# Windowed attention with sink tokens, then a token-and-channel mixer: a new start for the first batch (ones products, masks on TensorE, early sink rows) and a new order of loads

## The chip, the cores and the metric

The kernel runs on one core of one Trainium2 chip. The metric is the device time of one execution in microseconds (us), the median of several runs. Five engines work at once, each through its own list of instructions in order: PE (TensorE, matrix products), ACT (ScalarE), DVE (VectorE), POOL (GpSimd) and SP (SyncE, which here only issues transfers). Transfers are issued by SP (the hardware queue, q1 in the profile) and by POOL (the software queue, q0).

## The reference

Four batches, 8 heads, 768 positions, head size 64. Attention sees a window of 128 positions and 4 sink tokens. Its output, 768 x 512 per batch, goes through a mixer over tokens and one over channels.

```python
def _attn_ref(q, k, v, n_sink, window):
    scores = (1.0 / np.sqrt(D)) * np.matmul(q, k.transpose(0, 1, 3, 2))
    rel = pos[:, None] - pos[None, :]
    keep = (pos[None, :] < n_sink) | ((rel >= 0) & (rel < window))
    a = softmax(np.where(keep, scores, -1e9))
    return np.matmul(a, v)
def _moe_ref(x, w_tok1, w_tok2, w_ch1, w_ch2):
    h = np.maximum(x.transpose(0, 2, 1) @ w_tok1, 0.0) @ w_tok2
    u = x + h.transpose(0, 2, 1)
    return u + np.maximum(u @ w_ch1, 0.0) @ w_ch2
```

## The kernel before

**Pairs.** Heads are taken two at a time: 16 pairs, four per batch. SP loads q and k of a pair in fp32 (`load_qk`, line 72), POOL or, for pair 0, DVE casts them to bf16, and POOL issues the load of v (`load_v`, line 101), which casts in the transfer. PE transposes q and k (`transpose_q`, `transpose_k`, line 111) and ACT or DVE evicts the results, k in two halves (`kTz`), the second after the first. `score(p, kt)` makes the scores of one tile of 128 keys against 256 queries for both heads, ACT takes the exponential, and the window mask is applied in one of two ways: DVE multiplies the exponentials with 0 and 1 (line 390), or PE adds a large negative number first, by a product of the identity with `mask_add` (line 374). In the first four pairs the tiles with odd `kt` use the second way. `score_sinks` scores the 4 sink rows (`kTs`, copied out of `kTz`) and `pv` multiplies with v and, for the sinks, with `v_sinks`, which `sink_rows` copies out of v.

**Mixer.** `mix_h` and `mix_u` mix tokens; DVE adds x to the result of `mix_u` (line 538). For batch 0 PE transposes u (`transpose_u`); for the others a DMA does. `mix_channels` has 24 `v1` units per batch (product with w_ch1, then relu) and 24 `out_part` units (product with w_ch2, then an add and a store).

**Order.** All engines' lists are written by a planner before the kernel runs (`Plan.run`). It holds two streams of PE units: main (attention and token mixing of batch 0, then the channel mixing of all batches) and side (attention and token mixing of batches 1 to 3). Each stream keeps its own order. The planner has a cost for every unit and a due time for every load (`LANDED`), takes the stream that can begin, and keeps side at a pace given by `target`: side work of the next batch is to be done when 85% of the main work of a batch is (for the first from 20% on). The due times only decide the order that is written; on the chip each instruction waits for its real operands, and what stands behind it on its engine waits too.

**Loads.** POOL issues, in this order: v of pairs 0 and 1, the casts of pairs 1 and 2, v of pairs 2 and 3, the cast of pair 3, both token weights, the four parts of w_ch1. Pair p + 4 is loaded when `pv` of pair p is through (`load_next`); loads of q and k also wait until the last weight load so far has landed (`held`).

Of the kernel before, what the change touches and what calls it, by code (L numbers as in the profile page):

```python
# [16 lines left out]
def kernel(  # L17
# [77 lines left out]
    NV = 4  # L95
# [37 lines left out]


# [3 lines left out]
    mask_add = singles.tile([P, 2, 2, P], BF16)  # L138
# [21 lines left out]
    kTs = [singles.tile([P, 2, D], BF16, name=f"kTs{n}") for n in range(NKB)]  # L160

    v_sinks = [singles.tile([P, 2, D1], BF16, name=f"v_sink{n}") for n in range(NKB)]
    vs[0], _ = load_v(0)
    vs[1], _ = load_v(1)
    for n in range(NKB):
        e = (nc.vector, nc.gpsimd)[n]
        in_order(e.memset(kTz[n][D:P, 0], 0.0))
        in_order(e.memset(kTz[n][0:D, 1], 0.0))
        in_order(e.memset(kTs[n], 0.0))
        in_order(e.memset(v_sinks[n], 0.0))  # L170
    in_order(nc.vector.tensor_copy(out=mask_first, in_=mask_main))
    in_order(nc.vector.memset(mask_first[0:n_sink], 1.0))
    in_order(nc.vector.tensor_scalar(
        out=mask_add, in0=mask_main, scalar1=-1.0, scalar2=30000.0, op0=ALU.add, op1=ALU.mult,
    ))
# [21 lines left out]

    cast_qk(3)
    load_w(w_tok1, moe_w_tok1.rearrange("(t p) n -> p t n", p=P))
    load_w(w_tok2, moe_w_tok2.rearrange("(t p) n -> p t n", p=P))  # L200
    for n in range(NW):
        held = load_ch1(n)
# [22 lines left out]
    class Plan:  # L225
# [27 lines left out]
        def other(self):  # L253
            best = None
            for n, op in enumerate(self.pending):
                r = self.ready(op)
                if r is None:
                    continue
                e = min(op.cost, key=lambda e: max(self.free[e], r) + op.cost[e])
                t = max(self.free[e], r)  # L260
                if best is None or t < best[0] - 1e-6:
                    best = (t, n, e)
            return best
# [56 lines left out]
    def transpose_q(p):  # L320
        key = ("qT", p)

        def run():
            tiles["ps_q", p] = bank("mx", NT, P, dtype=BF16)
            for j in range(NT):
                transpose(tiles["ps_q", p][:, j], bfs[p][0][:, j])

        def evict(e):
            t = att_pool.tile([P, P, NT], BF16, name="qT2")
            copy(e, t, tiles["ps_q", p].rearrange("d j p -> d p j"))  # L330
            tiles[key] = t.rearrange("d p j -> d (p j)")

        done[key] = Op({"DVE": 950.0, "ACT": 900.0}, evict)
        return unit(340, run, [done["q_bf", p]], "mx", [done[key]])

    def transpose_k(p):
        kz, ks = kTz[p % NKB], kTs[p % NKB]

        def run():
            tiles["ps_k", p] = bank("mx", NT, P, dtype=BF16)  # L340
            for j in range(NT):
                transpose(tiles["ps_k", p][:, j], bfs[p][1][:, j])
            del bfs[p]

        def evict(i):
            return lambda e: copy(
                e, kz[ds(D * i, D), i].rearrange("d (p j) -> d p j", j=NT),
                tiles["ps_k", p][ds(D * i, D)].rearrange("d j p -> d p j"),
            )


        old = [done["sk", p - NKB]] if p >= NKB else []
        first = Op({"ACT": 800.0, "DVE": 950.0}, evict(0), old)
        second = Op({"ACT": 800.0, "DVE": 950.0}, evict(1), [first])
        sinks = Op({"ACT": 220.0, "DVE": 200.0}, lambda e: copy(e, ks[:, :, 0:n_sink], kz[:, :, 0:n_sink]), [second])
        tiles["kTz", p] = kz
        done["kT", p], done["kTs", p] = second, sinks
        done["kT0", p] = first
        return unit(340, run, [done["k_bf", p]], "mx", [first, second, sinks], [first, second])

    def score(p, kt):
# [3 lines left out]
        pe_mask = p < NHP and kt % 2 == 1  # L365
        tag = "mx" if p < NHP and kt % 2 else "sc"

        def run():
            if kt == 0:
                tiles["pT", p] = pt_pool.tile([P, NT, 2, 2, P], BF16, name="pT")  # L370
            ps_s = tiles["ps_s", p, kt] = bank(tag, 2, 2 * P)
            if pe_mask:
                mm(
                    ps_s[:, :, 0:nq * P].rearrange("p i (n q) -> p i n q", q=P), ident, mask_add[:, :, 0:nq],
                    start=True, stop=False,
                )
            for i in range(2):
                mm(
                    ps_s[:, i, 0:nq * P], tiles["kTz", p][:, i, ts(kt, P)], tiles["qT", p][:, kt * P:(kt + nq) * P],
                    start=not pe_mask, stop=True,  # L380
                )

# [14 lines left out]
        return unit(220 * nq * (1 if not pe_mask else 2) / 2, run, [done["qT", p], done["kT", p]], tag, then, [x])  # L397

    def score_sinks(p):
        def run():  # L400
            tiles["pT_sink", p] = pt_pool.tile([P, (NT - 2) * P], BF16, name="pT_sink")
            tiles["ps_sk", p] = bank("sc", (NT - 2) * P)
            mm(
                tiles["ps_sk", p], kTs[p % NKB].rearrange("p i c -> p (i c)"), tiles["qT", p][:, 2 * P:],
                start=True, stop=True,
            )
# [8 lines left out]
    def pv(p, half):  # L415
        b, hp = pairs[p]
        tag = "mx" if p < NHP and half else "pv"
        vsk = v_sinks[p % NKB]
# [33 lines left out]
        if half:  # L452
            done["pv", p] = op
            if p + NHP < len(pairs):
                op.then += load_next(p)
        return op

    def sink_rows(p):
        def both(e):
            for i in range(2):  # L460
                copy(e, v_sinks[p % NKB][D * i:D * i + n_sink, i], vs[p][0:n_sink, i, 0])

        done["vs", p] = Op({"ACT": 440.0, "DVE": 400.0}, both, [done["v", p]] + ([done["pv", p - NKB]] if p >= NKB else []))
# [61 lines left out]
    def mix_u(b, g, s0, n):  # L525
        c0, cn = group(b, g)

        def run():
            ps_u = tiles["ps_u", b, g, s0] = bank("mx", n, cn)
            for st in range(n):  # L530
                for tt in range(NTOK):
                    mm(
                        ps_u[:, st], w_tok2[:, tt, ts(s0 + st, P)], tiles["mix", b][0][:, tt, c0:c0 + cn],
                        start=(tt == 0), stop=(tt == NTOK - 1),
                    )

        def add(e):
            in_order(nc.vector.tensor_tensor(  # L538
                out=u_part(b, g, s0, n), in0=tiles["ps_u", b, g, s0],
                in1=x_sb[b][:, s0:s0 + n, c0:c0 + cn], op=ALU.add,  # L540
            ))

        op = Op({"DVE": 150.0 + 1.05 * n * cn}, add)
        done["u", b, g, s0] = op
        return unit(n * NTOK * cn * 0.422, run, done["h", b, g] + [done["tok2"]], "mx", [op])
# [34 lines left out]
    def attention_and_tokens(b):  # L580
        p0 = b * NHP
        units = [transpose_q(p0), transpose_k(p0)]
        for p in range(p0, p0 + NHP):
# [14 lines left out]
            units[-1].then.append(sink_rows(p))  # L598
# [4 lines left out]
        if b == 0:  # L603
            units += [mix_h(b, 0, 0, 1), pv(p, 0), mix_h(b, 0, 1, 1), pv(p, 1)]
            for st in range(NT):
                units.append(mix_u(b, 0, st, 1))
                if st >= 2:
                    units.append(transpose_u(b, 0, st - 2, 1))
            units += [
                mix_h(b, 1, 0, NTOK), transpose_u(b, 0, NT - 2, 1), mix_u(b, 1, 0, 4), transpose_u(b, 0, NT - 1, 1),  # L610
                mix_u(b, 1, 4, 2), transpose_u(b, 1, 0, 4), transpose_u(b, 1, 4, 2),
            ]
# [71 lines left out]
    def load_next(p):  # L684
        nxt = p + NHP

        def load_w2(n):
            def run(e):
                nonlocal held
                held = load_ch2(n)  # L690
            return run

        ops = []
        if 2 <= p < NHP:
            for n in (2 * p - 4, 2 * p - 3):
                done["ch2", n] = Op({"Q": 2500.0}, load_w2(n), [], lag=LOAD_LAG)
                ops.append(done["ch2", n])
        def load(e):
            nonlocal held
            raws[nxt] = load_qk(nxt, held if p < NHP else None)  # L700
            vs[nxt], held = load_v(nxt)
            bfs[nxt] = cast_tiles()

        def cast(n):
            return lambda e: copy("POOL", bfs[nxt][n].rearrange("p j h d -> p h j d"), raws[nxt][n])

        done["v", nxt] = Op({"Q": 4000.0}, load, [done["pv", p]] + ops, lag=LOAD_LAG)
        ops.append(done["v", nxt])
        for n, name in enumerate(("q_bf", "k_bf")):
            done[name, nxt] = Op({"POOL": 850.0}, cast(n), [done["v", nxt]])  # L710
            ops.append(done[name, nxt])
        return ops


    LANDED = {"q_bf": [0, 8400, 10500, 14700], "k_bf": [0, 9500, 12000, 15500], "v": [14400, 16500, 18000, 19000]}
    for n in LANDED:
        for p in range(NHP):
            done[n, p] = landed(float(LANDED[n][p]))
    done["tok1"], done["tok2"] = landed(21000.0), landed(23000.0)
    for n in range(NW):  # L720
        done["ch1", n] = landed(26000.0 + 2500.0 * n)

    plan = Plan()
    plan.free.update(PE=3000.0, ACT=2200.0, DVE=3900.0, Q=30000.0)
    raw0 = raws.pop(0)
    for n, (name, at) in enumerate((("q_bf", 3900.0), ("k_bf", 5100.0))):
# [4 lines left out]
        plan.pending.append(done[name, 0])  # L731

# [14 lines left out]
    def target(m):  # L747
        m -= first
        total = 0.0
        for n, (msize, ssize) in enumerate(sizes):  # L750
            begin = 0.2 if n == 0 else 0.0
            f = (m / msize - begin) / (0.85 - begin)
# [44 lines left out]
```

## Time and profile before

| | |
|---|---|
| median of 3 runs | 227.07 us (226.96 to 228.21) |
| the profiled execution | 226.43 us, span 224.7 us |
| PE busy | 203.8 us (91%) |
| DVE, ACT, POOL busy | 130.1, 123.3, 53.0 us |
| granted TensorE clock | 1.000 (mean) |
| DMA moved | 28.59 MB, mean 127 GB/s |

The span runs from the first to the last instruction of the core; the profiled execution's own time is 1.7 us longer than its span, and 0.6 us under the median. Durations below are of this one execution. A matrix product is shown until its result is written, so products in a row overlap: what a product costs in a row of them is the distance from start to start. L108 and L111 are the lines of helpers (`mm`, `transpose`), so rows are told apart by their tiles: `ps_sc` and `ps_mx` are PSUM tiles, `pT` the exponentials, `u_sb` the mixed tokens, `o_sb` the output.

### The profile page before, as it was taken

The numbers are of one execution on the slowest core, as the hardware profiler recorded it, in microseconds if no ns is written. First come the engines' busy times: TensorE is split into PE (matmuls) and PEld (weight loads), VectorE is DVE, ScalarE is ACT, GpSimd is POOL, SyncE is SP. The second block draws the span as 40 slices with busy tenths as digits, with TensorE's granted clock in tenths as the row PEclk, the third lists the DMA queues.
The fourth block names the chain that finished last, engine by engine and source line by source line (L and its number), as shares of the span: only waits on it lengthen the run. The fifth ranks groups of instructions, "written<-read, shape, count | busy, mean of one in ns | idle before, by whom it ended". The sixth has DMA issues, their size and how long they took to land.

```text
span 224.7 us, 4298 instructions
## 1 busy us (share of the span) xinstructions
PE 203.8 (91%) x1716; PEld 131.5 (59%) x1716; DVE 130.1 (58%) x286; ACT 123.3 (55%) x248; POOL 53.0 (24%) x70
## 2 busy tenths in 40 slices
PE   1787897997996999699999999999999999999992
PEld 1456565674664656467776665667765664565440
DVE  6388974165997764468966544679846643000321
ACT  2788945895881511799872510889954311774000
POOL 8798106602534035000440152000000000000000
PEclk9999999999999999999999999999999999999999
DMA  6999997998977399940552999100004124100222
GB/s 195 311 188 155 203 192 238 159 162 282 303 44 100 74 252 271 247 147 3 36 35 48 266 226 166 74 0 3 0 3 117 47 96 117 47 3 0 93 95 93
DMA packets 51284, 28.59 MB, mean 127 GB/s; under 512 B 35392, under 2 KB 48192, under 8 KB 51264
## 3 DMA queue, kind: packets, MB, share of 16 engines
q0 software_dynamic: 29600, 7.08, 33.6%
q1 hardware_dynamic: 21664, 21.24, 30.6%
q8 instruction: 13, 0.21, 0.4%
q14 instruction: 7, 0.06, 0.1%
HBM read 26.74 MB, written 6.29 MB: 147 GB/s over the span
## 4 chain that ended last, share of the span: by engine, by line
PE 76%; DMA 11%; DVE 5%; ACT 4%; issue 1%; POOL 1%; SPq 0%; POOLq 0%
PE ps_mx L108 60%; PE ps_sc L108 8%; DMA w_ch<-in_moe_w_ch_dram 5%; PE ps_pv L108 5%; PE ps_mx L111 4%; DMA k_f<-in_k_dram 4%; ACT kTz L115 3%; DMA q_f<-in_q_dram 2%; DVE kTs L117 2%; DVE kTz L117 1%; ACT pT L384 1%; DVE o_sb L653 1%; DVE x_sb L440 0%; SPq L72 0%; POOL q_bf L117 0%
## 5 line engine op out<-in xcount | busy, mean ns | idle before, releaser
L108 PE MATMUL ps_mx<-uT,w_ch 128*128 128x384 bf16 x384 | 69.2, 326 | 0.0
L108 PE MATMUL ps_mx<-w_ch,v1T 128*128 128x512 bf16 x288 | 68.8, 379 | 0.0
L384 ACT ACTIVATE pT<-ps_sc 128x512 bf16<-128x512 f32 x84 | 45.7, 566 | 20.0 <-PE ps_sc L108 19.2
L108 PEld LDWEIGHTS <-w_ch 128*128 128x128 bf16 x384 | 36.7, 98 | 20.5
L108 PEld LDWEIGHTS <-v1T 128*128 128x128 bf16 x288 | 27.4, 98 | 26.2
L121 ACT ACTIVATE v1T<-ps_mx 128x384 bf16<-128x384 f32 x67 | 32.7, 491 | 16.1 <-PE ps_mx L108 8.1
L653 DVE TENSOR_TENSOR o_sb<-ps_mx,u_sb 128x512 f32<-128x512 f32 x24 | 16.5, 687 | 42.6 <-PE ps_mx L108 42.6
L108 PE MATMUL ps_sc<-qT,kTz 128*128 128x256 bf16 x168 | 30.4, 270 | 6.4 <-ACT kTz L115 3.6
L101 POOL DMA_DIRECT2D v_aug<-in_v_dram x16 | 16.9, 1056 | 55.6 <-ACT pT L384 19.1
L390 DVE TENSOR_TENSOR pT<-pT,mask_main 128x512 bf16<-128x512 bf16 (+1 forms) x68 | 28.7, 434 | 1.9 <-ACT pT L384 1.3
L108 PEld LDWEIGHTS <-kTz 128*128 128x128 bf16 x192 | 17.9, 101 | 18.3 <-ACT kTz L115 5.4
L123 DVE TENSOR_SCALAR v1T<-ps_mx 128x384 bf16<-128x384 f32 x29 | 16.1, 555 | 13.5 <-PE ps_mx L108 13.2
L108 PEld LDWEIGHTS <-w_tok 128*128 128x128 bf16 x192 | 17.7, 98 | 8.0 <-issue 2.7
L538 DVE TENSOR_TENSOR u_sb<-ps_mx,x_sb 128x512 bf16<-128x512 f32 (+2 forms) x26 | 15.4, 643 | 10.1 <-PE ps_mx L108 10.1
L108 PEld LDWEIGHTS <-pT 128*128 128x128 bf16 x352 | 16.8, 97 | 2.9 <-issue 0.7
L121 ACT ACTIVATE h1T<-ps_mx 128x512 bf16<-128x512 f32 (+2 forms) x9 | 5.0, 550 | 24.3 <-PE ps_mx L108 24.3
L115 ACT ACTIVATE kTz<-ps_mx 64x768 bf16<-64x768 bf16 x20 | 16.1, 802 | 1.4 <-PE ps_mx L111 0.6
L108 PE MATMUL ps_pv<-v_aug,pT 128*128 128x65 bf16 x304 | 16.3, 194 | 0.0
L115 ACT ACTIVATE qT<-ps_mx 128x768 bf16<-128x768 bf16 x9 | 7.3, 812 | 16.0 <-PE ps_mx L111 16.0
L440 DVE TENSOR_TENSOR x_sb<-ps_pv,recip 128x384 bf16<-128x384 f32 x28 | 15.5, 553 | 0.6
L117 POOL CAST q_bf<-q_f 128x768 bf16<-128x768 f32 x12 | 10.0, 834 | 24.7 <-DMA q_f<-in_q_dram 24.7
L111 PE MATMUL ps_mx<-ident,q_bf 128*128 128x128 bf16 x96 | 8.7, 231 | 6.9 <-DVE q_bf L117 4.5
(59 smaller groups left out, 192.2 us busy)
## 6 DMA issues: line engine op xcount, KB each, us to landing
q_f<-in_q_dram SPq DMA_DIRECT2D x16, 384.0 KB, 4.6
k_f<-in_k_dram SPq DMA_DIRECT2D x16, 384.0 KB, 5.4
out_dram<-o_sb SPq DMA_DIRECT2D x24, 256.0 KB, 2.2
v_aug<-in_v_dram POOLq DMA_DIRECT2D x16, 192.0 KB, 6.0
w_ch<-in_moe_w_ch_dram POOLq DMA_DIRECT2D x8, 384.0 KB, 8.9
w_tok<-in_moe_w_tok_dram POOLq DMA_DIRECT2D x2, 384.0 KB, 6.0
uT<-u_sb SPq DMA_TRANSPOSE x9, 3.2
```

Of the source, the lines that this page charges most:

```text
L101: d = in_order(nc.gpsimd.dma_start(out=v_aug.rearrange("p i t d -> p (i t) d")[:, :, 0:D], in_=v[b].rearrange("h s d -> (h s) d")[2 * hp * ...
L108: in_order(nc.tensor.matmul(*args, skip_group_check=True, **kwargs))
L111: in_order(nc.tensor.transpose(out, in_, ident))
L115: in_order(nc.scalar.activation(out, in_, AF.Copy))
L117: in_order({"DVE": nc.vector, "POOL": nc.gpsimd}[e].tensor_copy(out=out, in_=in_))
L121: in_order(nc.scalar.activation(out, in_, AF.Relu))
L123: in_order(nc.vector.tensor_scalar_max(out=out, in0=in_, scalar1=0.0))
L384: in_order(nc.scalar.activation(tiles["pT", p][:, kt, :, 0:nq], tiles["ps_s", p, kt][:, :, 0:nq * P], AF.Exp, scale=scale,))
L390: in_order(nc.vector.tensor_tensor(out=pt, in0=pt, in1=msk[:, :, 0:nq], op=ALU.mult))
L440: in_order(nc.vector.tensor_tensor(out=x_sb[b][:, ts(half, QH), ts(hp, 2 * D)].rearrange("p t (i d) -> p t i d", i=2), in0=tiles["ps_o", p ...
L538: in_order(nc.vector.tensor_tensor(out=u_part(b, g, s0, n), in0=tiles["ps_u", b, g, s0], in1=x_sb[b][:, s0:s0 + n, c0:c0 + cn], op=ALU.add,))
L653: in_order(nc.vector.tensor_tensor(out=o_sb.rearrange("p (g c) -> p g c", g=2), in1=u_rows(b, st), in0=tiles["ps_out", b, st].rearrange("p ...
```

## The change

- A tile of ones is set by DVE at the start, and PE multiplies it with itself (products of 512 columns, no reader): 7 times ahead of all work, 3 times behind the transposes of q of pair 0, 4 times behind those of k, once behind each of the six `score` units of pair 0.
- All score tiles of the first four pairs are masked by PE, and tile 1 of pair 4. The masks for it are made by DVE after the start (`mask_rest`).
- The sink rows of k and v of the four pairs of batch 0 are loaded by four small transfers on POOL's queue, two behind v of pair 0 and two behind v of pair 1. PE transposes the sink rows of k (`transpose_sinks`, in the main stream behind `transpose_k` of pair 0 and ahead of `score(0, 0)`). The copies out of `kTz` and v are dropped for these pairs.
- In three of six `mix_u` units of batch 0's first column group PE adds x by a product with the identity, and ACT or DVE only copies; the units of batch 0's token mixing stand in another order.
- Six buffers for v instead of four. Pair 4 is loaded behind the token weights, ahead of w_ch1, pair 5 behind w_ch1; later pairs by a queue of their own order, w_ch2 behind pair 6.
- The pace of the side stream: from 0% to 60% of the main work, for every batch.

The diff, cut to its core:

```diff
+    ones = singles.tile([P, 4 * P], BF16)
+    in_order(nc.vector.memset(ones, 1.0))
+    def keep_warm(n):
+        for _ in range(n):
+            mm(bank("mx", 4 * P), ones[:, 0:P], ones, start=True, stop=True)
+    keep_warm(7)
...
+    in_order(nc.vector.memset(k_sink0, 0.0))
+    in_order(nc.vector.memset(v_sink0, 0.0))
     vs[0], _ = load_v(0)
+    for i in range(2):
+        rows = slice(D * i, D * i + n_sink)
+        in_order(nc.gpsimd.dma_start(
+            out=k_sink0[rows, :, i], in_=k[0].rearrange("(p i) s d -> i s p d", i=2)[i, 0:n_sink],
+        ))
     vs[1], _ = load_v(1)
-    for n in range(NKB):
-        e = (nc.vector, nc.gpsimd)[n]
-        in_order(e.memset(kTz[n][D:P, 0], 0.0))
...
+    for i in range(2):
+        rows = slice(D * i, D * i + n_sink)
+        in_order(nc.vector.memset(v_sink0[rows, :, i, D:D1], 1.0))
+        in_order(nc.gpsimd.dma_start(
+            out=v_sink0[rows, :, i, 0:D], in_=v[0].rearrange("(p i) s d -> i s p d", i=2)[i, 0:n_sink],
+        ))
...
+    tok1_landed = load_w(w_tok1, moe_w_tok1.rearrange("(t p) n -> p t n", p=P))
     load_w(w_tok2, moe_w_tok2.rearrange("(t p) n -> p t n", p=P))
+    raws[NHP] = load_qk(NHP, tok1_landed)
+    vs[NHP], _ = load_v(NHP)
+    ch1_landed = [load_ch1(n) for n in range(NW)]
+    raws[NHP + 1] = load_qk(NHP + 1, ch1_landed[1])
+    vs[NHP + 1], held = load_v(NHP + 1)
...
+    def transpose_sinks():
+        def run():
+            ps = tiles["ps_ks"] = bank("mx", NHP, P, dtype=BF16)
+            for n in range(NHP):
+                transpose(ps[:, n], k_sink0[:, n].rearrange("p i d -> p (i d)"))
+        op = Op({"ACT": 590.0, "DVE": 420.0}, lambda e: copy(e, kTs0.rearrange("p n i d -> p n (i d)"), tiles["ps_ks"]))
...
+        return unit(224, run, [landed(8000.0)], "mx", [op])
...
-        pe_mask = p < NHP and kt % 2 == 1
+        pe_mask = p < NHP or kt == 1 and p == NHP
...
+                if by_pe:
+                    mm(ps_u[:, st], ident, x_sb[b][:, s0 + st, c0:c0 + cn], start=True, stop=False)
...
-        units = [transpose_q(p0), transpose_k(p0)]
+        units = [transpose_sinks()] if b == 0 else []
+        units = [transpose_q(p0), transpose_k(p0)] + units
...
-    LANDED = {"q_bf": [0, 8400, 10500, 14700], "k_bf": [0, 9500, 12000, 15500], "v": [14400, 16500, 18000, 19000]}
+        "v": [14700, 16300, 17800, 19200, 25000, 35500], "vs": [9500] * NHP,
+        "raw": [0] * NHP + [26000, 36500],
...
-            begin = 0.2 if n == 0 else 0.0
-            f = (m / msize - begin) / (0.85 - begin)
+            begin = 0.0
+            f = (m / msize - begin) / (0.6 - begin)
```

## The prediction

> **What bounds the kernel now.** I read the page first: PE is busy 91% of the span and its clock is granted in full, so the kernel is PE work plus the places where PE waits. The busy time by stage shows where these lie (columns: busy us and count of PE, PEld, DVE, ACT, POOL, then clock, DMA share, GB/s).
>
> ```profile
> 0.00:5.00 5.00, 0.51 (x6) 0.52 (x6) 3.15 (x14) 1.28 (x1) 4.16 (x12) 1.00 0.60 186
> 5.00:10.00 5.00, 3.50 (x22) 2.16 (x21) 1.36 (x4) 3.62 (x5) 4.13 (x8) 1.00 1.11 306
> 15.00:20.00 5.00, 3.25 (x42) 2.41 (x42) 4.58 (x11) 3.88 (x11) 5.00 (x7) 1.00 1.50 125
> 35.00:40.00 5.00, 3.85 (x43) 2.73 (x41) 2.34 (x6) 3.06 (x5) 4.05 (x6) 1.00 0.66 191
> 180.00:200.00 20.00, 20.00 (x122) 11.83 (x121) 4.51 (x7) 8.06 (x17) 0.00 (x0) 1.00 0.24 72
> ```
>
> PE loses time mostly in the first 40 us; later it is nearly always busy. The chain of waits names what stands there (start, us, what).
>
> ```profile
> 6.34 0.80 ACT kTz L115
> 7.17 0.81 ACT kTz L115
> 8.03 0.40 PE ps_sc L108
> ...
> 13.73 0.30 PE ps_sc L108
> ...
> 19.54 11.88 DMA w_ch<-in_moe_w_ch_dram
> ...
> 36.77 0.84 POOL k_bf L117
> ```
>
> Scores of pair 0 start at 8.0, of pair 1 at 13.7, then (timeline) of pair 2 at 19.5, of pair 3 at 24.2, the first `v1` unit at 38.0. Behind 45 us PE's waits are these (total, times, longest):
>
> ```profile
> PE ps_sc L108 <- ACT kTz L115: 2.3, 3, 1.3
> PE ps_mx L108 <- DVE x_sb L440: 1.7, 1, 1.7
> PE ps_mx L111 <- POOL q_bf L117: 1.5, 1, 1.5
> PE ps_sc L108 <- ACT pT L384: 0.5, 1, 0.5
> ```
>
> That is 6.0 us. From 38.0 to the last product at 220.65 there are so 182.65 - 6.0 = 176.6 us of PE work, which the change hardly touches.
>
> Last, the transfers. v of pair 0 is issued at 2.51 and lands 11.8 us later, at 14.3; here are it and two issued near 20 us (KB, us to landing):
>
> ```profile
> v_aug<-in_v_dram POOLq DMA_DIRECT2D x1, 192.0 KB, 11.8
> ...
> w_ch<-in_moe_w_ch_dram POOLq DMA_DIRECT2D x1, 384.0 KB, 11.9
> v_aug<-in_v_dram POOLq DMA_DIRECT2D x1, 192.0 KB, 12.8
> ```
>
> The software queue q0 works in order: the last two were issued at 19.5 and 20.3 and landed at 31.4 and 33.1, the smaller behind the larger, though a v takes 6.0 us in the page's median. By the queue's packets per microsecond, q0 moves none before 7.6, then some 200 per us beside q1's q and k, and the 1536 packets of pair 0's v are through at about 13.1.
>
> **The change, part by part. The sink rows.** Their two k transfers are queued on q0 behind v of pair 0, so by that order their packets move at about 13.1 and land no earlier than that v. DVE sets the ones first (0.48 us, as `mask_main`), so `mask_main`, POOL's selects and this v shift by 0.45: it lands at 14.75, the sink rows at 14.8. Bounds: 2 us behind their issue, about 8 (if small transfers overtook), and 16.3 (behind pair 1's v, which lands at 16.1 now). The nearest rows, every pair of loads in q0, say in order; I take 14.8. `transpose_sinks` reads them and stands on PE ahead of `score(0, 0)`. Queued behind it on PE is everything, so scores of pair 0 begin at about 15.2, not 8.0; ACT and DVE then wait for PE.
>
> The Trainium skill, "DMA: Bandwidth & Descriptors", section "Anatomy of one DMA — SWDGE (gpsimd) path", fits 2.0 us plus bytes over 436 GB/s per transfer: 2 us for these rows, 2.9 for a v, where the trace has 11.8 behind a full start. By that fit the sinks would be there at 8 us; the sum by it is the first rival's.
>
> **Ones products.** Cold, 512 columns take 0.42 us (the mask product at 8.22, the next at 8.64), warm 0.21 (13.85 to 14.06). Seven run from 1.55 to 4.5, beside the load of q; three behind q's transposes (0.64 to 1.28) may hold k's by up to 0.7 us, and four lie under the evictions of k (1.6 us). All of this is over by 7.5 us and hidden by the wait to 14.8: cost nothing here, without that wait 0 to 0.7. But PE then stands still for 7 us. After the 4.5 idle us at the start it was slow (six transposes 0.64, later 0.34), and became fast after about 4.8 us of work without a break from 8.0. No later break is as long, so whether 7 us make it slow again lies between nothing and all of it; the start is the nearest row, I take all. Slow work from 14.8 to about 19.9: sinks 0.43, then each score unit 0.85 with its mask and 0.42 for its ones; two of these, transposes 0.64, a third: 19.7. Then fast: 0.65, transposes 0.34, so 20.7; k of pair 1 is evicted in two halves of 0.8 to 0.96, and pair 1's scores start at 22.7: **+9.0** against 13.7. Fast throughout it would be +6.5, slow for another 2 us +10.
>
> On the clock, the Trainium skill, "TensorE: Matmul & The Clock Gate", Part 1, has half rate return after an idle window of about 3.4 us, which would settle the open bound on my side.
>
> **Masks on PE.** Twelve more mask products, 0.21 each warm: 0.64 us of PE per pair (0.43 for its tiles 0 and 2 ahead of the transposes of the next k). DVE loses three products per pair (0.42 each), and the copies of sinks (0.2 plus 0.37 to 0.5 a pair) go, one of which PE waited 0.6 us for at 15.0. From the start of a pair's scores: four score units 1.5, transposes 0.67, `pv` 0.36, write 0.2, queueing on DVE 0.2, two serial halves with their signals 1.9: 4.9 us per pair, where pair 1 took 5.8 and pair 2 4.7.
>
> **End of batch 0.** PE work from pair 3's scores to `v1`: scores, sinks, `pv` of pair 2 3.3, first `mix_h` and `pv` of pair 3 2.9, rest of the mixing 4.6 (5.1 with three x products of 3 x 0.16), and about 1.1 us of last evictions: 12.4, against 13.8 (24.2 to 38.0), in which PE stood 1.0 for pair 4's q. Sum from pair 1's scores: 4.9 + 4.9 + 12.4 = 22.2 against 24.3: **-2.1**. With pair 4's q, k and v loaded first, side units fill gaps there: I take 1.3 us of PE work against 0.66 now: **-0.6**; bounds 0 and -2.
>
> **Loads.** w_ch1 lands up to 3.2 us later (a pair's 0.96 MB ahead of it, at some 300 GB/s); the first part landed at 25.7, `v1` starts after 36: hidden, and each part feeds 3.9 us of PE. w_ch2, now after pair 6 at some 50 us, is needed past 60: hidden; if not, it costs its lateness. POOL: four small issues (0.2 to 0.76 each, a memset and a `w_tok` issue being the nearest rows) replace memsets of 2.1 us: 2.0, no change for the casts.
>
> **Later.** The pair-6 wait (1.5) goes with six v buffers and earlier loads. The 1.7 us on x_sb follow a copy of 8 columns on DVE that took 3.51 us beside four POOL casts in a row (67.1 to 70.2); with casts earlier it goes. The 2.3 us are starts of batches, where main had to wait for u; with side done at 60% main can run there. Against it: ACT and DVE were busy 31.6 of 40 us in 100:120 and the attention now falls more densely; two new us of waits. **-4.0**, bounds -5.5 and +1. One mask product in pair 4: +0.2.
>
> **Sum.** 9.0 - 2.1 - 0.6 - 4.0 + 0.2 = +2.5, so 226.4 (the profiled execution: span 224.7 plus 1.7) becomes 228.9; the median lies 0.6 higher: **229.6**.
>
> **Rivals.** *Sinks in time (faster).* The small transfers don't queue behind v and land by about 8.5. Price: the 9.0 shrink to 0.2, since pair 1's scores then start near 13.9 and PE reaches `pv` of pair 0 as its v lands (14.75), and the sum is -6.3: 221; with half of the gain in the later waits 223. For it speaks that nothing in the trace shows a transfer of a few rows behind a large one; against it, every landing in q0's order. It decides if the rows land before 8.5; each us beyond costs one.
> *Late, but paid back.* Sinks late, yet PE stays fast over the wait (-2.5), or the later waits vanish whole: 225 to 227.5. Against it is the slow start of PE at 4.5.
> *The ones don't warm PE.* With sinks in time but slow products to 13 us, three masks (1.3) and six ones (2.5) lengthen pair 0 by 3.8: 224.8. The rows at 8.0 to 13 show that steady work does warm it, so I give it little, within the first rival.
>
> **How the numbers follow.** Sinks late, slower: 0.54, 229.6, alone 227 to 233. Sinks in time: 0.32, 221 to 225. Paid back: 0.14. A measurement of this kernel can tell about 0.5% (1.1 us) from no change. Faster (under 225.9): 0.30 of the first rival, 0.06 of the paid back, 0.02 of the forecast: 0.38. Slower (over 228.2): 0.46 of the forecast and 0.01 of the rest: 0.47; 0.15 between. Range 220.3 to 233: below lies the best quarter of the first rival, 0.08, above 0.07 of the forecast.
>
> **What would show it.** Right: PE idle from about 7 to 14.8, ended by a transfer into `k_sink`; scores of pair 0 at 15.2, of pair 1 near 22.7, `v1` near 45, waits behind it of 2 us. Wrong: `transpose_sinks` before 9, a start of pair 1 near 14, or `v1` by 37.

## The result, and the profile after

The kernel after takes 228.65 us (median of 20 runs, 227.41 to 229.57) beside 226.47 us of the kernel before on the same chips (20 runs, 224.46 to 229.19): a ratio of 1.0113 [1.0086, 1.0141], so 1.1% slower. Ratios, here and below, are taken from fast runs alone and need not be the quotients of the medians beside them, which are of all runs. The profiled execution of the kernel after took 229.29 us with a span of 227.6, against 226.43 and 224.7: the span grew by 2.9. Every span below is that of one profiled execution; the 20 executions of the kernel after had spans of 225.5 to 227.8, so a difference of 1 us between two spans shows little.

First the busy time by stage, as it was read for the kernel before (columns: busy us and count of PE, PEld, DVE, ACT, POOL, then clock, DMA share, GB/s).

```profile
5.00:10.00 5.00, 3.36 (x19) 1.80 (x16) 2.45 (x6) 2.45 (x3) 3.93 (x6) 1.00 1.06 314
10.00:15.00 5.00, 0.00 (x0) 0.00 (x0) 0.00 (x0) 0.00 (x0) 4.32 (x6) 0.58 1.64 221
15.00:20.00 5.00, 3.90 (x19) 2.41 (x20) 0.50 (x2) 1.19 (x2) 5.00 (x7) 0.50 1.67 122
20.00:25.00 5.00, 4.54 (x33) 2.79 (x33) 2.79 (x3) 3.15 (x6) 2.93 (x4) 0.90 1.56 188
```

From 10 to 15 us PE, DVE and ACT do nothing at all. Then 3.9 us of PE time hold only 19 rows, where the kernel before did 42 in less: the granted clock is 0.50. PE cooled while it stood, which means here that its granted clock fell to half. The chain of waits (start, us, what) names the cause and shows how the slowness ends.

```profile
3.10 1.09 POOL v_aug L101
4.20 0.78 POOL k_sink L182
4.97 10.99 DMA k_sink<-in_k_dram
16.10 0.59 PE ps_mx L111 x4
16.69 0.85 PE ps_sc L108 x3
17.54 1.71 PE ps_mx L108 x5
19.25 0.64 PE ps_mx L111 x6
...
21.82 0.35 PE ps_mx L111 x6
```

The sink rows of k, issued behind v of pair 0, landed 11.0 us after their issue, at 16.0. Six transposes took 0.64 us at 19.25 and 0.35 at 21.82: the first were slow, the second fast. The DMA issues between 3 and 6 us (KB, median us to landing) show how little the size counted:

```profile
v_aug<-in_v_dram POOLq DMA_DIRECT2D x2, 192.0 KB, 12.0
k_sink<-in_k_dram POOLq DMA_DIRECT2D x2, 2.0 KB, 11.2
```

By the timeline scores of pair 0 start at 16.7, of pair 1 at 24.19, of pairs 2 and 3 at 28.82 and 33.69, and the first `v1` unit at 47.18 (before: 8.0, 13.73, 19.54, 24.22 and 38.0). So `v1` is 9.2 us late and the span only 2.9: over six us come back later. PE's waits, first of the whole execution, then behind 45 us (total, times, longest):

```profile
PE ps_mx L111 <- DMA k_sink<-in_k_dram: 7.7, 1, 7.7
...
```

```profile
PE ps_sc L108 <- ACT kTz L115: 0.5, 1, 0.5
PE ps_sc L108 <- ACT pT L438: 0.5, 1, 0.5
PE ps_mx L108 <- DVE x_sb L494: 0.3, 1, 0.3
```

That is 1.3 us behind 45, where there were 6.0.

### The profile page after: what moved, and what is told of

Its sections match the earlier page's. It is cut to its first block, busy times and chain, and to the rows that moved or that the text cites. A ratio compares the mean times of both kernels' runs of the same rounds, so it can differ in the third digit from the quotient of the medians.

```text
span 227.6 us, 4342 instructions
## 1 busy us (share of the span) xinstructions
PE 210.6 (93%) x1738; PEld 135.6 (60%) x1756; DVE 130.3 (57%) x285; ACT 117.0 (51%) x233; POOL 52.5 (23%) x70
## 4 chain that ended last, share of the span: by engine, by line
PE 83%; DMA 5%; DVE 5%; ACT 3%; issue 2%; POOL 1%; ACTq 0%
PE ps_mx L108 64%; PE ps_sc L108 9%; PE ps_pv L108 5%; DMA k_sink<-in_k_dram 5%; PE ps_mx L111 5%; DVE kTz L117 2%; ACT kTz L115 1%; ACT pT L438 1%; DVE o_sb L710 1%; DVE x_sb L494 0%; POOL v_aug L101 0%; DVE qT L117 0%; DVE kTs L117 0%; POOL k_sink L182 0%; POOL mask_main L156 0%
## 5 line engine op out<-in xcount | busy, mean ns | idle before, releaser
L108 PE MATMUL ps_mx<-w_ch,v1T 128*128 128x512 bf16 x274 | 65.0, 379 | 0.7
L121 ACT ACTIVATE v1T<-ps_mx 128x384 bf16<-128x384 f32 x67 | 32.8, 491 | 18.1 <-DVE o_sb L710 9.8
L108 PE MATMUL ps_sc<-qT,kTz 128*128 128x256 bf16 x168 | 29.6, 268 | 2.3 <-DVE kTz L117 0.9
L444 DVE TENSOR_TENSOR pT<-pT,mask_main 128x512 bf16<-128x512 bf16 (+1 forms) x59 | 26.3, 457 | 1.0 <-ACT pT L438 0.5
L117 POOL CAST q_bf<-q_f 128x768 bf16<-128x768 f32 x12 | 10.0, 830 | 36.8 <-DMA q_f<-in_q_dram 15.5
L117 DVE COPY qT<-ps_mx 128x768 bf16<-128x768 bf16 x13 | 12.4, 955 | 10.2 <-PE ps_mx L111 10.1
L595 DVE TENSOR_TENSOR u_sb<-ps_mx,x_sb 128x512 bf16<-128x512 f32 (+2 forms) x23 | 14.0, 655 | 6.3 <-PE ps_mx L108 6.2
L115 ACT ACTIVATE kTz<-ps_mx 64x768 bf16<-64x768 bf16 x19 | 15.2, 801 | 2.6 <-PE ps_mx L111 1.8
L494 DVE TENSOR_TENSOR x_sb<-ps_pv,recip 128x384 bf16<-128x384 f32 x28 | 15.5, 554 | 0.5
L117 DVE COPY kTz<-ps_mx 64x768 bf16<-64x768 bf16 x13 | 12.4, 955 | 1.7 <-PE ps_mx L111 1.3
```

Source lines behind the costliest of these rows:

```text
L108: in_order(nc.tensor.matmul(*args, skip_group_check=True, **kwargs))
L115: in_order(nc.scalar.activation(out, in_, AF.Copy))
L117: in_order({"DVE": nc.vector, "POOL": nc.gpsimd}[e].tensor_copy(out=out, in_=in_))
L121: in_order(nc.scalar.activation(out, in_, AF.Relu))
L444: in_order(nc.vector.tensor_tensor(out=pt, in0=pt, in1=msk[:, :, 0:nq], op=ALU.mult))
L494: in_order(nc.vector.tensor_tensor(out=x_sb[b][:, ts(half, QH), ts(hp, 2 * D)].rearrange("p t (i d) -> p t i d", i=2), in0=tiles["ps_o", p ...
```

## The experiments

The theory: the sink rows come late behind v in the software queue, PE stands and cools, and the rest of the change gives part back. The rival from the prediction: with the rows in time the kernel would be faster than before, about 221. "v1" below is the start of the first `v1` unit.

### One suspect at a time

**Sink rows of k at the head of the queue.** Those of v go behind v of pair 0.

```diff
-    vs[0], _ = load_v(0)
     for i in range(2):
         rows = slice(D * i, D * i + n_sink)
         in_order(nc.gpsimd.dma_start(
             out=k_sink0[rows, :, i], in_=k[0].rearrange("(p i) s d -> i s p d", i=2)[i, 0:n_sink],
         ))
-    vs[1], _ = load_v(1)
+    vs[0], _ = load_v(0)
     for i in range(2):
         rows = slice(D * i, D * i + n_sink)
         in_order(nc.vector.memset(v_sink0[rows, :, i, D:D1], 1.0))
         in_order(nc.gpsimd.dma_start(
             out=v_sink0[rows, :, i, 0:D], in_=v[0].rearrange("(p i) s d -> i s p d", i=2)[i, 0:n_sink],
         ))
+    vs[1], _ = load_v(1)
```

> The changed kernel, with the two small loads of k's sink rows issued ahead of v of pair 0 and v's sink rows behind it. My theory (the sink rows wait in the software queue behind v of pair 0, and PE waits for them): they land by about 6 to 8 us, PE's wait of 7.7 us for k_sink falls to under 1, pair 1's scores begin near 15 in place of 24.2, and as v of pair 0 is issued 1.4 us later PE may wait for it until about 16; time 7 to 8 us below the changed kernel, 221 against 226.5 for the kernel before. Rival (software-queue transfers do not start before about 8 us whatever their order): rows at 9 to 10, PE still waits 1.5 us, 222 to 223. Rival (the wait only shows what is lost elsewhere anyway): 227 to 229.

Measured: 225.03 us, ratio to before 0.9966 [0.9921, 1.0011]; span 223.5. The DMA issues and PE's waits of this run:

```profile
k_sink<-in_k_dram POOLq DMA_DIRECT2D x2, 2.0 KB, 7.0
```

```profile
PE ps_mx L111 <- DMA k_sink<-in_k_dram: 2.8, 1, 2.8
```

Issued at 3.05 and 3.8 with nothing ahead of them, 2 KB still took 6.8 to 7.3 us and landed near 11.1, and the 2.8 us of wait were enough to cool PE:

```profile
10.00:15.00 5.00, 3.81 (x21) 2.32 (x22) 0.66 (x2) 1.19 (x2) 4.48 (x6) 0.66 1.72 217
```

Pair 1 starts at 18.40 (in the kernel after: 24.19) and v1 at 41.85 (47.18). The queue's order was the cause of most of the wait; it is worth some 1.5% by the ratios, 3.3 us (the two spans differ by 4.1). The rest of the wait stays because 2 KB at the head of the queue come some 7 us after their issue. The time is a miss: 221 was expected, and 222 to 223 by the rival that came nearest, which had the rows at 9 to 10 us and no cooling behind a wait of 1.5.

**No early sink rows: the copies from `kTz` and v again.** All else is kept as changed; the four small transfers go too.

```diff
-    in_order(nc.vector.memset(k_sink0, 0.0))
+    in_order(nc.vector.memset(kTs0, 0.0))
...
-        if p < NHP:
-            sinks = done["kTs", p]
-        else:
+        if True:
             sinks = Op({"ACT": 220.0, "DVE": 200.0}, lambda e: copy(e, ks[:, :, 0:n_sink], kz[:, :, 0:n_sink]), [second])
...
-        units = [transpose_sinks()] if b == 0 else []
+        units = []
...
-            if b:
-                units[-1].then.append(sink_rows(p))
+            units[-1].then.append(sink_rows(p))
```

> The changed kernel without the early sink loads: sink rows are copied out of kTz and v again, as in the kernel before, all else as changed. My theory: no wait of PE at the start, pair 1's scores near 14, the copies cost 0.2 plus 0.4 us of DVE or ACT a pair, partly on the path; about 221.5 against 226.5 before, so that the early sink loads alone cost about 7 us. Rival (the loss comes from the ones products or the masks on PE): 227 or more.

Measured: 226.88 us, ratio 1.0052 [1.0007, 1.0096]. This is the miss that matters. No wait for the sinks' loads is left (0.9 us for the copy of v's sink rows is) and pairs 1 to 3 start at 14.25, 20.87 and 25.75, yet v1 only at 43.13. PE's waits between 15 and 40 us begin so:

```profile
PE ps_mx L111 <- POOL k_bf L117: 1.6, 1, 1.6
PE ps_mx L111 <- POOL q_bf L117: 1.6, 1, 1.6
```

The side stream now reaches pair 4, whose q and k the planner expects at 26.0. They could be cast only at some 30 to 32 us. What the late sinks had hidden became the next wait. This execution kept the full clock (mean 1.000); the nine others have means of 0.983 to 0.992, so PE cooled in them as well, at a place that no trace of them shows.

**PE kept busy through the wait.** The second group of ones products is made long enough.

```diff
-                keep_warm(4)
+                keep_warm(44)
```

> The changed kernel with 44 ones products behind k's transposes instead of 4, so that PE works through its wait for the sink rows. My theory (PE falls back to half speed in the wait and pays for it until about 21 us): granted clock 1.0 from 10 to 25 us, pair 1's scores at 21.5 to 22 in place of 24.2, 2 to 2.5 us below the changed kernel, about 226.3. Rival (the slow products hide behind ACT): within 0.5 us of the changed kernel.

Measured: 227.37 us, ratio 1.008 [1.0046, 1.0114].

```profile
10.00:15.00 5.00, 5.00 (x25) 2.25 (x23) 0.00 (x0) 0.00 (x0) 4.49 (x6) 1.00 1.77 234
15.00:20.00 5.00, 5.00 (x42) 3.25 (x40) 1.77 (x3) 2.39 (x4) 5.00 (x7) 1.00 1.92 152
```

Products of ones with ones hold the clock at 1.00, and 42 rows fit between 15 and 20 us instead of 19. Pair 1 starts at 21.61, 2.6 us earlier, of which 0.2 go to the sinks' transposes, which start at 15.92 instead of 16.10; so the cooling costs 2.4 us of the first 10.5 (the prediction had charged 2.5). The place was as expected, the time was not: 2 to 2.5 us less were expected, the spans differ by 1.6, and by the ratios, whose intervals overlap, it is 0.7. The rest is given back later.

**No ones products at all.**

```diff
-    keep_warm(7)
...
-                keep_warm(3)
...
-                keep_warm(4)
...
-                keep_warm(1)
```

> The changed kernel without any ones products. My theory: as the wait for the sink rows lets PE cool anyway, the ones before it do nothing, and the six inside pair 0 cost 0.43 us each while slow and 0.22 when fast: pair 1's scores 1.5 to 2 us earlier, about 226.8. Rival (the ones shorten the slow time): the same as the changed kernel or slower, 228.7 to 230.

Measured: 227.79 us, ratio 1.0081 [1.0044, 1.0118]. Pair 1 starts at 20.89, 3.3 earlier, of which 1.5 go to the sink rows, which landed at 14.5 in this execution; PE is slow for 3.2 us of work there, not 4.9, and does not have the six ones of pair 0 to make. The time lies between what was expected and the rival, and its interval overlaps that of the kernel after: beside this wait the ones bring nothing that can be told.

**The sinks' transposes moved to just ahead of their first reader**, `score_sinks(0)`; the queue's order is kept.

```diff
-        units = [transpose_sinks()] if b == 0 else []
-        units = [transpose_q(p0), transpose_k(p0)] + units
+        sinks_unit = [transpose_sinks()] if b == 0 else []
+        units = [transpose_q(p0), transpose_k(p0)]
...
-            units += [score(p, 5), score_sinks(p)]
+            units += [score(p, 5)] + (sinks_unit if p == 0 else []) + [score_sinks(p)]
```

> The changed kernel with transpose_sinks moved on PE from ahead of pair 0's scores to just ahead of score_sinks(0); the loads stay in their order. My theory (the loss is the place on PE of an instruction that waits for a late load): PE does pair 0's six score units from about 9 to 13 and waits only from there to 16; pair 1's scores near 17.5 in place of 24.2, v1 near 42; as in the run with the sink rows first, part of it is given back to the loads of pair 4 (q and k usable at 31 to 33): about 225 against 226.1 before. Rival (late landing costs the same wherever it is waited for): 228 to 229.

Measured: 225.98 us, ratio 0.9963 [0.992, 1.0007]. Six score units now run ahead of the rows, which still come near 16: the wait is 3.3 us instead of 7.7, and cools PE as well. Pair 1 starts at 18.1 and v1 at 43.37.

```profile
PE ps_mx L111 <- DMA k_sink<-in_k_dram: 3.3, 1, 3.3
```

```profile
15.00:20.00 5.00, 3.28 (x17) 1.97 (x18) 0.42 (x1) 1.54 (x3) 5.00 (x7) 0.55 1.48 102
20.00:25.00 5.00, 4.72 (x51) 3.30 (x49) 3.27 (x6) 2.98 (x6) 3.50 (x5) 0.77 1.53 184
```

### The wait taken away whole

**Both edits: rows first, transposes last.**

> Both: k's sink rows issued first and transpose_sinks just ahead of score_sinks(0), so that no wait for sinks is left at the start. If that wait alone were the loss: pair 1's scores near 14.5 and 3 us less than the run with the rows first, 222. My theory now (behind the sinks stands the load of v of pair 0, landing near 16, and then that of pair 4, whose transposes stand on PE ahead of batch 0's mixing and are usable at 30 to 33 only): PE waits 3 to 5 us for q_bf and k_bf near 28 to 33, and the time stays within 1 us of the run with the rows first, 224.5 to 225.5.

Measured: 228.24 us, ratio 1.0057 [1.0017, 1.0097]. No wait for the sinks' loads is left, pairs 1 to 3 start at some 14, 18.67 and 23.55, about as early as in the kernel before or earlier, and it is no faster than before. The wait that was expected came, near its size; the time, expected at 224.5 to 225.5, missed. PE's waits between 15 and 40 us, and two windows:

```profile
PE ps_mx L111 <- POOL k_bf L117: 2.6, 1, 2.6
PE ps_mx L111 <- POOL q_bf L117: 2.0, 1, 2.0
```

```profile
25.00:30.00 5.00, 2.42 (x32) 1.61 (x30) 1.76 (x4) 2.46 (x6) 0.83 (x1) 1.00 1.20 266
30.00:35.00 5.00, 2.96 (x19) 1.96 (x20) 1.36 (x2) 0.98 (x2) 0.83 (x1) 0.70 1.53 224
```

4.6 us for pair 4's q and k, a clock of 0.70 behind them, and v1 at 43.95, later than in the run that kept a 2.8 us wait. The gain went to the next late load.

**Copies, and truer due times for pairs 4 and 5.**

```diff
-        "raw": [0] * NHP + [26000, 36500],
+        "raw": [0] * NHP + [31000, 37500],
```

> The run with copied sink rows, and the planner's due times of q and k of pairs 4 and 5 set from 26.0 and 36.5 us to 31.0 and 37.5, near what the traces show; loads and work are the same, only the order written for PE changes: the transposes of pair 4 move behind the first mix_h units. My theory (4.7 us of PE's waits there are for q_bf and k_bf): these go, time 2 to 3 us less than with the old due times (226.9), about 224.3. Rival (the work missing there is made up later anyway): no change within 0.7 us.

Measured: 229.09 us, ratio 1.011 [1.0019, 1.0201]: missed again (four runs). Pair 4's waits are gone and v1 starts at 39.29. But PE cooled early here, behind two short waits of 0.74 us (v of pair 0, until 15.70) and 0.77 us (the copy of its sink rows, until 16.81):

```profile
15.00:20.00 5.00, 3.53 (x25) 2.36 (x25) 2.25 (x6) 2.20 (x4) 5.00 (x8) 0.68 1.67 120
```

Pair 2 starts 8.3 us behind pair 1, where the run with copies and the old due times took 6.6 with much the same two waits and a clock of 1.00. And there is a loss one load further on: pair 7's q and k are issued only when w_ch2 has landed (54.0), and between 40 and 80 us PE has this wait:

```profile
PE ps_mx L111 <- POOL q_bf L117: 3.1, 1, 3.1
```

Behind it the six transposes of k at 61.41 take 0.85 us as one group, not the 0.50 of a fast one. The prediction asked of w_ch2 only when it is needed itself, and called it hidden; the loads that are held until it has landed were not priced.

**The loads put in the order in which they are needed.** The two edits of the sinks; a longer planned time for a pair's load (4.0 to 6.5 us), a later one at which the queue is free, later due times for pairs 4 and 5, and w_ch2 behind pair 7 instead of pair 6:

```diff
-        return Op({"Q": 4000.0}, load, [("pv", n - NV), ("q_bf", n - NHP), ("k_bf", n - NHP)], lag=LOAD_LAG)
+        return Op({"Q": 6500.0}, load, [("pv", n - NV), ("q_bf", n - NHP), ("k_bf", n - NHP)], lag=LOAD_LAG)
...
-        "raw": [0] * NHP + [26000, 36500],
+        "raw": [0] * NHP + [31000, 39500],
...
-    plan.free.update(PE=3000.0, ACT=2200.0, DVE=3900.0, Q=36500.0)
+    plan.free.update(PE=3000.0, ACT=2200.0, DVE=3900.0, Q=38000.0)
...
-        if n == 2 * NHP - 2:
+        if n == 2 * NHP - 1:
```

> k's sink rows issued first, transpose_sinks just ahead of score_sinks(0), and the loads behind it in the order of need: w_ch2 behind pair 7 instead of behind pair 6, and the planner's due times for pairs 4 to 7 set to what the traces show (31.0 and 39.5 us for pairs 4 and 5, 6.5 us a pair from 38 on). My theory (every wait removed so far was handed on to the next load, and each wait of 3 us or more also cooled PE): no wait of PE over 1 us between 5 and 60 us, clock 1.0 throughout, v1 near 39, 3 to 5 us below the kernel before: ratio 0.98 to 0.985. Rival (the transfers of the first 60 us bound the start, whatever their order): waits of 3 us and more remain, ratio 0.995 to 1.005.

Measured: 222.41 us beside 226.72, ratio 0.9864 [0.98, 0.9928], just short of the 0.98 to 0.985 that was expected. This version beats both kernels. Which of the edits to the loads and due times it needs was not tried apart. Its two windows beside those of the kernel after:

```profile
10.00:15.00 5.00, 4.48 (x41) 3.01 (x39) 2.33 (x3) 4.07 (x8) 4.61 (x7) 1.00 1.87 226
15.00:20.00 5.00, 4.72 (x68) 3.63 (x66) 3.26 (x6) 4.34 (x9) 5.00 (x7) 1.00 1.97 162
```

PE is busy and the clock full. Pairs start at some 14, 19.04 and 23.91, v1 at 36.16, the span is 219.7. PE's waits of the whole execution begin with the first tile of ones, and then no group sums to over 1.3 us (between 5 and 60 us none to over 0.8):

```profile
PE ps_mx L108 <- DVE ones L135: 1.5, 1, 1.5
PE ps_sc L108 <- ACT kTz L115: 1.3, 3, 0.5
PE ps_mx L108 <- DVE x_sb L494: 1.1, 1, 1.1
PE ps_mx L111 <- ACT k_bf L115: 0.7, 1, 0.7
```

### What the other parts are worth

**The reordered version without ones products.**

> The same without any ones products. With no long wait left, the ones should now pay: without them pair 0 runs slow until about 13 us (0.85 us a score unit) and pair 1's scores begin 0.5 to 2 us later; but v of pair 0 lands near 15 to 16 and may hide that. I expect 0 to 1 us more than with them. Rival (the ones only lengthen PE's list): 0.5 to 1 us less.

Measured: 222.67 us, ratio 0.9875 [0.9812, 0.9937]; v1 at 36.28. Products of 512 columns are slow there until some 11.5 us, but that start is not what the batch waits for. No gain from the ones can be told.

**The reordered version with masks on PE for odd tiles only**, as in the kernel before.

```diff
-        pe_mask = p < NHP or kt == 1 and p == NHP
+        pe_mask = p < NHP and kt % 2 == 1
```

> The reordered kernel with the masks of the first four pairs as before: only tiles with odd kt on PE, the others by DVE. If masks on PE help (DVE loses three products of 0.42 us a pair), the distance between the starts of pairs grows from 4.9 us to 5.2 or more and the time by 1 to 1.5 us. If the chain of scores, transposes and the two evictions of k bounds a pair, as I reckoned (the extra 0.43 us of PE is on it, DVE is not), the distance is 4.7 to 4.9 and the time the same within 1 us. I expect the second.

Measured: 222.46 us, ratio 0.9816 [0.9762, 0.9871]; pairs start at 14.31, 19.54 and 24.34, v1 at 36.35. The starts are 5.2 and 4.8 us apart; the time is the same, as expected. The intervals overlap: no gain or loss from putting all masks on PE can be told.

**The kernel after with the old pace of the side stream.**

```diff
-            begin = 0.0
-            f = (m / msize - begin) / (0.6 - begin)
+            begin = 0.2 if n == 0 else 0.0
+            f = (m / msize - begin) / (0.85 - begin)
```

> The changed kernel with the side stream's old pace (20% to 85% of the main work for the first batch, 0 to 85% later). If the pace is what removed 4.7 us of PE's waits behind 45 us, about 3 to 4 us of waits at the starts of batches come back: 231 to 232. If the earlier loads and six v buffers did it, within 1 us of the changed kernel, 228.5 to 229.5. I expect half of it: 230.

Measured: 231.4 us, ratio 1.021 [1.0138, 1.0281], span 229.2. PE's waits behind 45 us begin with

```profile
PE ps_sc L108 <- ACT kTz L115: 2.3, 3, 1.3
```

which is the prediction's 2.3 us at the starts of batches, in the same three parts (1.26, 0.55 and 0.47 us). They were charged to the old pace, and with it they return: 231 to 232 was the time named for that, 230 the one expected. By the ratios the pace is worth 1.0% here, over four runs whose interval just touches that of the kernel after; the spans differ by 1.6 us. The waits on x_sb and on pair 6's q do not return with it.

**The kernel before with the new pace alone.**

> The kernel before with only the new pace of the side stream (0 to 60%). In the changed kernel the old pace brought back 2.3 us of waits on kTz; if the pace alone is worth that, 2 us less than before (ratio 0.991). If the denser side stream meets the old loads (four v buffers, pair loads behind pv), PE waits for q_bf of pairs 5 to 7 grow from 1.5 us to 3 or more and it is the same or slower: ratio 1.0 to 1.01. I expect the second.

Measured: 225.08 us, ratio 0.9954 [0.9911, 0.9997]. A miss, in the mechanism too: it was expected to be the same or slower, with more waiting for q_bf of pairs 5 to 7. Behind 45 us PE's waits are 2.3 us, not 6.0: those on x_sb and on pair 6's q are gone with the old loads, while 1.8 of the 2.3 us on `kTz` stay. Ahead of that, the wait for pair 4's q grows from 1.0 us to 1.9 in this execution, and PE cools behind it (a clock of 0.84 and 0.82 in the two windows from 35 to 45 us). One line of the change does by itself what the whole change did not, though by little.

## Why the prediction was right, and where it was not

The forecast was 229.6 us, slower, +2.5 on the median known then; measured were 228.65, slower, +2.2 between the medians of 20 runs. Its sum stands so, in the profiled executions:

| term | predicted | measured | from |
|---|---|---|---|
| pair 1's scores | +9.0 | +10.5 | 24.19 against 13.73 |
| pair 1 to `v1`, side work in the gaps included | -2.1 - 0.6 | -1.3 - 1.4 | 47.18 - 24.19 = 23.0 against 24.3; some 2.1 us of side work in it against 0.66 |
| waits behind 45 us | -4.0 | -4.7 | 1.3 against 6.0 |
| mask of pair 4 | +0.2 | not seen apart | |
| sum | +2.5 | about +3 | span +2.9 |

**The mechanism was right.** The rows queued behind v, `transpose_sinks` held all that stands behind it on PE, PE cooled in the wait and warmed in steady work, and two thirds of the loss at `v1` (9.2 us, of which 2.9 are left) came back later. The runs with the rows first and with the transposes last show the first two, the one with PE kept busy the third, the one with the old pace a part of the fourth. Of the rival *Late, but paid back* the first half failed, PE did not stay fast, and the second came only in part: 1.3 of 6.0 us of waits are left, which is nearer to the forecast's 2.0 than to none.

**Mis-sized: the first term, by 1.5.** The rows were to land at 14.8 and landed at 16.0: v of pair 0 came at 15.45 and not at 14.75 (12.4 us from an issue at 3.05), and the rows 0.5 behind it and not 0.05. That makes 1.2 us; the rest is the 0.14 us from the landing to the first transpose, and slower transposes of the sinks, 0.59 for 0.43. In the four other runs with this order of loads the rows landed at 14.4 to 16.1, so 14.8 lies within what executions differ by. What followed had been sized well: PE was slow for 4.9 us of work, from 16.1 to some 21.0, where the prediction had 5.1. The Trainium skill's fit ("DMA: Bandwidth & Descriptors", "Anatomy of one DMA — SWDGE (gpsimd) path"), 2.0 us plus size, does not describe these transfers: 11.0 us behind a v, 6.0 to 7.3 at the head of the queue. The Trainium skill's idle window of about 3.4 us ("TensorE: Matmul & The Clock Gate", Part 1) gave the right answer for 7.7 us of wait; here 2.8 and 3.3 us cooled PE already, with a mean clock of 0.66 and 0.55 in the 5 us that hold the end of the wait.

**Mis-split: the next two terms, right in sum.** PE did more side work in batch 0 than the 1.3 us that had been taken, and the stage was longer by as much; both sums are -2.7.

**Wrong: the price of the rival *Sinks in time*.** Two steps failed. Its condition was rows by 8.5 us; the runs show that no place in the queue gives that: at its head, issued from 3.05 us on, both rows have landed only at 10.2 to 11.1. And its price, 221, took away one wait and kept all else. With the wait away (by copies, or by both edits of the sinks) ratios were 1.0052 and 1.0057: pair 4's q and k, for which the sum had no wait, and then pair 7's, held behind a w_ch2 that **Loads** calls hidden, were next, and the longer of these waits cooled PE. Only with the loads in order too came about what the rival had named: `v1` at 36.16, where its start of pair 1 (13.9) and the stage of 22.2 give 36.1, and a span 5.0 us under that of the kernel before where its sum had 6.3; by the ratio it is 3.1 of 226.7. The rival *The ones don't warm PE* fell with the run that kept PE busy, but so did the use of the ones: without them the time is the same.

**Wrong, at no cost:** "no change for the casts". The first cast of pair 1 starts at 8.62, not 7.49. The four small issues, of 0.57 to 0.79 us, end at 7.76, and then POOL waits 0.86 us for q of pair 1 to land; why that came later is not shown. PE was waiting for the sinks all the while. **Later** held in size: of its 6.0 us 1.0 stayed (0.5 on `pT`, 0.5 on `kTz`), and of the two new us that it set against the gain 0.3 came. Of its causes only one is shown, and in part: with the new loads the pace removes 1.8 of the 2.3 us at the starts of batches, with the old loads only 0.5. The waits on x_sb and on pair 6's q are gone with the new pace and old loads and with the old pace and new loads, so six v buffers, earlier loads and earlier casts are not shown to be what removed them.

## What to carry to other kernels

Look at what stands behind an instruction on its in-order engine before giving it a load of its own: two transfers of 2 KB that only the last scores of a pair need held up everything on PE from 8.4 to 16.1 us, because their transposes stood first. When a wait of several us is priced, follow the work that it delays to the next load it will meet, with the landing times in the trace and not the planner's: twice here the removed wait reappeared at a load that the old wait had covered. A change of many parts can be slower as a whole while its parts, put in the order of need, are 1.4% faster. Look at the clock of every execution before an explanation is built on one trace: the traced execution of the run with copies was the only one of ten at the full clock.

## What the runs showed of the hardware that was not expected

- The software queue's first transfers landed 6.0 to 7.3 us after issue even with 2 KB and nothing ahead (five runs with the rows first); no packet of this queue moved before 7.2 to 8.4 us in any run.
- Waits of 7.7, 2.8 and 3.3 us on PE halved its granted clock, which fell at some 10.8, 10.9 and 15.5 us, about 2.5 us after PE had stopped. Two waits of 0.74 and 0.77 us close together did so in one run (copies with later due times, clock 0.68 from 15 to 20 us), while 0.49 and 0.94 us at the same place did not in another (copies, 1.00), so the length of one wait does not decide it. Products of ones kept the clock at 1.00 through 7 us.
- The kernel before cools in some executions too: of the 17 beside the reordered version six have a mean clock of 0.992 and spans of 225.1 to 226.4 us, the others 0.999 or 1.000 and 222.7 to 225.4.
- The granted-clock column reads 1.00 over the first microseconds although products run at half speed there: in the kernel before a product of 512 columns takes 0.63 us at 8.22 and 0.38 at 13.85. Without ones it reads 1.00 from 10 to 20 us, while the four transposes of the sinks at 14.56 take 0.58 us, as in the kernel after at a clock of 0.50 (0.59), and not 0.39 as in the run with PE kept busy. So here the column shows a fall of the clock, and not that PE starts slow.
